# Reading back a block of Z in three transfers instead of two: 48 rows on SP's queue, 4 rows on GpSimd's

## The chip, the core and the metric

The kernel runs on one core of a Trainium2 chip. The metric is the device time of one execution, in microseconds (us), as the median of several runs. A core has engines that run side by side: TensorE (PE, with weight loads shown as PEld), VectorE (DVE), ScalarE (ACT), GpSimd (POOL) and SyncE (SP). Each has a queue of its own instructions in program order. Transfers are issued from SP's or from GpSimd's queue here, and they are carried out by 16 DMA engines that both queues share.

## What is computed

The reference chains two layers. The first is a long causal convolution of `x` (8 batches, 5696 positions, 128 channels) with a filter `h` for each channel, by FFT of twice the length. The second takes that result's first 64 frequencies through a complex matrix each, transforms back, adds, and applies a channel matrix with a ReLU:

```
Xf = rfft(x, n=2S);  Hf = rfft(h, n=2S);  y = irfft(Xf * Hf, n=2S)[:, :S]      # S = 5696
X  = rfft(y);  Y[:, m] = X[:, m] @ (w_r[m] + i w_i[m])  for m < 64, else 0
u  = y + irfft(Y, n=S)
out = u + max(u @ w_ch, 0)
```

## The kernel before

The transform of length S is split as 64 x 89. The batches go in four pairs `g_`. For each pair, the first part of the kernel transforms `x`, multiplies it with the filter's spectrum and applies the short inverse transform. What comes out, called Z, has 180 rows (90 frequencies, a real and an imaginary row each), 64 positions, and 2 x 128 columns (two batches by channels), in 16-bit floats. The function `tick` does four frequencies at a time and writes each step's Z to a scratch tensor in HBM (`zscr`) from SP's queue; the transfers carry the token `("zd", g_, s_)`. It also keeps sums for the 64 modes of the second layer.

The second part of the kernel reads Z back in blocks. A block is one pair and 16 of the 64 positions: 180 rows of 8192 bytes. There are 16 blocks. As an SBUF tile has 128 partitions, a block is two tiles: `zt[i % NC][0]` with rows 0 to 127, and `zt[i % NC][1]` with the other `RB` = 52 rows, which lie in partitions 32 to 83 (`PB` = 32). Five blocks have a buffer at a time (`NC` = 5); the profile calls them ZT0a, ZT0b to ZT4a, ZT4b.

- `load_zt` (L527 to 533) reads one block: a transfer for each part, both on SP's queue, on the semaphores of the ring `"t"`. It waits until what lay in the buffer's memory before is no longer read: in the first round older tensors (`zt_old`), later PE's matmuls on the block that had the buffer.
- `clear_zt` (L535) sets partitions 0 to 31 of the second tile to zero on GpSimd, once for each buffer, since PE reads its partitions 0 to 83.
- The first four blocks are loaded during the last pair's ticks, by the table `early` (L558 to 565): memset 0 at tick 9, load 0 at tick 10, memset 1 at tick 14, load 1 at tick 16, load and memset 3 at tick 19, load and memset 2 at tick 21. After the last tick come `load_wi` (two small transfers on GpSimd's queue, the tile WI), then load and memset 4. Block `i + 5` is loaded when block `i` has been used (L923).
- `u_z` (L782) has PE multiply a block with the transform's last matrix: for each of 16 positions and two batches a matmul with the first part and one with the second, 89 columns wide, accumulated in PSUM. `u_c` (L809) adds the second layer's contribution in a 356-column matmul (tiles IBs, C). `u_tile` copies the sum to the tile UT on ACT or DVE.
- `o_tile` (L866) multiplies UT with `w_ch` and the identity (tile WI, four 256-column matmuls), ACT takes the ReLU into R, DVE adds it into an output buffer O (seven of them of 512 KB, two tiles each) or Os, and SP's queue stores it to `out`. The main loop (L913) interleaves blocks and output tiles: while PE works on one pair's blocks, output tiles of the pair before are made.

The order of the work comes from a recorder (`Recorder`). Each instruction names the tokens that it reads and writes; the recorder works out which earlier instructions it must wait for, and puts the waits ahead of it on its engine. A transfer's semaphore comes from a ring of a fixed length (`"t"` 20, `"q"` 10; the ring `"q"` exists before the change and is not used). Waiting holds up all that stands behind on the same queue. The helpers `dma` (L319) and `mm` (L322) record transfers and matmuls, so that most rows of the profile carry L320 and L323, and it is the tile names that tell them apart.

Of the kernel before, what the change touches and what calls it, by code (L numbers as in the profile page):

```python
# [4 lines left out]
P = 128  # L5
# [118 lines left out]
def bass_long_conv_fft__then__afno_spectral_mix_kernel(nc, x, h, moe_w_r, moe_w_i, moe_w_ch, out):  # L124
# [10 lines left out]
    NT = (NK + KT - 1) // KT  # L135
# [22 lines left out]
    s4 = np.stack([back[:, None, None] * np.cos(ang), -back[:, None, None] * np.sin(ang)], axis=0)  # L158
    RB, PB = 2 * NK - P, 32
# [46 lines left out]
    def at(name, cols, dt, off):  # L206
        return nc.alloc_sbuf_tensor_at(name, [P, cols], dt, offset=off)
# [49 lines left out]
    NC = 5  # L257
    ZP = ZB * 2 * D
# [5 lines left out]
    zt = [[at(f"ZT{i}{'ab'[p_]}", ZP, F16, zt_off[i][p_]) for p_ in range(2)] for i in range(NC)]  # L264
# [27 lines left out]
    def pv(bank, off, dims, p0=0, n=P):  # L292
        return bass.AP(ps, p0 * 4096 + bank * 512 + off, [[4096, n]] + [list(d) for d in dims])
# [5 lines left out]
    def bank(i):  # L299
        return ("bank", i)  # L300
# [18 lines left out]
    def dma(eng, dst, src, ring, reads=(), writes=(), after=()):  # L319
        R.add(eng, lambda h_: h_.dma_start(dst, src), reads, writes, ring=ring, after=after)  # L320

    def mm(o, l, r, st, sp, reads, writes):  # L322
        R.add("tensor", lambda h_: h_.matmul(o, l, r, start=st, stop=sp), reads, writes)  # L323
# [3 lines left out]
    def once(key, toks):  # L327
        if key in first:
            return []
        first[key] = 1  # L330
        return list(toks)
# [3 lines left out]
    def turns(name, items):  # L335
        i = ring2.get(name, 0)
        ring2[name] = i + 1
        return items[i % len(items)]
# [102 lines left out]
    for j in range(16):  # L441
        t = turns("h", [0, 2, 4])
# [11 lines left out]
        if j % 2:  # L454
            i = j // 2 % 2 * XC + j // 4
# [69 lines left out]
    zt_old = [(H_ALL, H_ALL), (AST, AST), (AST, AST), (H_ALL, H_ALL), (M_ALL[3:6], G_ALL)]  # L525

    def load_zt(i):  # L527
        g_, c_ = divmod(i, J // ZB)
        for part, (p0, r0, n) in enumerate(((0, 0, P), (PB, P, RB))):
            old = list(once(("zt", i % NC, part), zt_old[i % NC][part]))  # L530
            dma("sync", bass.AP(zt[i % NC][part], p0 * ZP, [[ZP, n], [1, ZP]]),
                bass.AP(zs, (g_ * 2 * NK + r0) * J * 256 + c_ * ZB * 256, [[J * 256, n], [1, ZP]]),
                "t", [("zd", g_, s_) for s_ in range(NT)], [("zt", i % NC, part)], after=old)

    def clear_zt(i):  # L535
        z32 = zt[i][1][0:PB, :].bitcast(U32)
# [14 lines left out]
    def load_s4(part):  # L551
# [6 lines left out]
    early = {3: lambda: load_w(2), 5: lambda: load_w(3), 8: lambda: load_s4(1),  # L558
             9: lambda: clear_zt(0),
             10: lambda: load_zt(0),  # L560
             12: lambda: load_s4(0),
             14: lambda: (load_id(), load_ib(), clear_zt(1)),
             16: lambda: load_zt(1),
             19: lambda: (load_zt(3), clear_zt(3)),
             NT - 2: lambda: (load_zt(2), clear_zt(2))}
    pace = []
# [211 lines left out]
    NCH = J // ZB  # L778
# [3 lines left out]
    def u_z(i, b, half, alone=False, parts=(0, 1)):  # L782
        g_, c_ = divmod(i, NCH)
        t = ahead.get((i, b, half))
        if t is None:
            t = turns("l", LSLOT)
        z = zt[i % NC]
        for hb in parts:
            if not alone:
                u_c(i, b, half, t, hb, True)  # L790
            for pl in range(4):
                for ri in range(2):
                    pz = half * 8 + hb * 4 + pl
                    so = (c_ * ZB + pz) * NQ
                    n = (P, PB + RB)[ri]
                    mm(pv(t + hb, pl * NQ, [[1, NQ]]), z[ri][0:n, pz * 256 + b * P:pz * 256 + b * P + P], s4_sb[ri][0:n, so:so + NQ],
                       alone and pl == 0 and ri == 0, not alone and pl == 3 and ri == 1, [("zt", i % NC, ri), ("zt0", i % NC), ("s4", ri, 0)] + ([("s4", ri, 1)] if c_ >= NCH // 2 else []), [bank(t + hb)])
        if alone:
            ahead[(i, b, half)] = t
        return t  # L800

    def u_c(i, b, half, t, hb, first_):
        g_, c_ = divmod(i, NCH)
        pl0 = half * 8 + hb * 4
        mm(pv(t + hb, 0, [[1, 4 * NQ]]), c_sb[:, (2 * g_ + b) * P:(2 * g_ + b + 1) * P],
           ib_sb[:, (c_ * ZB + pl0) * NQ:(c_ * ZB + pl0 + 4) * NQ], first_, not first_,
           [("c", g_ // 2), ("ib", 0)] + ([("ib", 1)] if c_ >= NCH // 2 else []), [bank(t + hb)])

    def u_tile(i, b, half):  # L809
        g_, c_ = divmod(i, NCH)  # L810
        t = ahead.get((i, b, half))
        if t is None:
            t = u_z(i, b, half)
        else:
            for hb in range(2):
                u_c(i, b, half, t, hb, False)
        ub = (g_ % 2) * 2 + b
        old = {0: WT, 1: WT, 2: U_ALL, 3: U_ALL}[ub]
        n_ev[0] += 1
        e = "scalar" if n_ev[0] % 8 in (0, 2, 3, 5, 7) or g_ == NP - 1 else "vector"  # L820
        src = pv(t, 0, [[1, NQ], [512, 2], [NQ, 4]])
        evac(bass.AP(u_sb[ub], c_ * ZB + half * 8, [[S, P], [J, NQ], [4, 2], [1, 4]]),
             src, [bank(t), bank(t + 1)], [("u_", ub, 2 * c_ + half)], eng=e, after=once(("u", ub), old))
# [6 lines left out]
    def mix(m0, m1):  # L830
        for m in range(m0, m1):
            for ri, first_col in ((0, (3 * m + 1) * B), (1, 3 * m * B)):
                n = min(MC, 32 - m % 32)
                mm(pv(6 + m // 32, m % 32 * 2 * B, [[1, 2 * B * n]]), w_sb[:, (ri * M + m) * D:(ri * M + m + 1) * D],
                   bass.AP(xt, first_col, [[B * XTW, P], [0, n], [1, 2 * B]]), ri == 0, ri == 1, WT + XTT, [bank(6 + m // 32)])

    u_z(0, 0, 0, True)
    for n in range(2):
        mix(16 * n, 16 * n + 16)
        u_z(0, 0, 1, True, (n,))  # L840
    mix(32, M)
    u_z(0, 1, 0, True, (0,))
    for hb in range(2):
        evac(bass.AP(y_sb, hb * 32 * B, [[2 * M * B, P], [B, 32], [M * B, 2], [1, B]]),
             pv(6 + hb, 0, [[2 * B, 32], [B, 2], [1, B]]), [bank(6 + hb)], [("y", hb)], eng="vector" if hb else "scalar",
             after=ZY)
# [66 lines left out]
    for g_ in range(NP):  # L913
        last = g_ == NP - 1
        order = [(c_, b) for b in range(2) for c_ in range(NCH)] if last else [(c_, b) for c_ in range(NCH) for b in range(2)]
        for n, (c_, b) in enumerate(order):
            i = NCH * g_ + c_
# [46 lines left out]
```

## Time and profile before

| what | value |
|---|---|
| runs, median of 3 | 378.18 us (377.16 to 381.03) |
| the profiled execution's own time | 379.06 us |
| its span | 377.3 us |
| granted TensorE clock, mean | 0.995 |
| PE busy | 359.0 us, 95% of the span |
| DVE, ACT, POOL busy | 295.1, 314.7, 75.4 us |
| moved by DMA | 103.94 MB, mean 276 GB/s |
| issues for blocks of Z | 32, all on SP's queue: 16 of 1024 KB, 16 of 416 KB |

The span runs from the first to the last instruction of one profiled execution, and the execution's own time holds what lies around it too. In the timeline, the line of an issue gives the time that the issue took on its queue; the time to landing is given apart, where the profile can find it. A wait is put down to what released it; "issue" stands where the profile can't tell. Busy time of PE is modelled for matmuls that overlap, so two matmuls' starts say more than their durations.

In the span, the transform of the filter and of the first inputs takes the first 40 us or so, and the four pairs follow. The last writes of Z are issued from 262.50 us on, within 3.33 us. Blocks of Z are issued from 236.85 to 327.92 us, PE reads them from 257.1 to 364.4 us, and the last store is issued at 373.8 us.

### The profile page before, as it was taken

The numbers are of one execution on the slowest core, as the hardware profiler recorded it, in microseconds if no ns is written. First come the engines' busy times: TensorE is split into PE (matmuls) and PEld (weight loads), VectorE is DVE, ScalarE is ACT, GpSimd is POOL, SyncE is SP. The second block draws the span as 40 slices with busy tenths as digits, with TensorE's granted clock in tenths as the row PEclk, the third lists the DMA queues.
The fourth block names the chain that finished last, engine by engine and source line by source line (L and its number), as shares of the span: only waits on it lengthen the run. The fifth ranks groups of instructions, "written<-read, shape, count | busy, mean of one in ns | idle before, by whom it ended". The sixth has DMA issues, their size and how long they took to land.

```text
span 377.3 us, 12488 instructions
## 1 busy us (share of the span) xinstructions
PE 359.0 (95%) x5370; PEld 279.0 (74%) x5370; DVE 295.1 (78%) x336; ACT 314.7 (83%) x495; POOL 75.4 (20%) x117
## 2 busy tenths in 40 slices
PE   7989989999999999999999999999999999999994
PEld 7878856666866666866667856667899989888873
DVE  3548889998898999998998988873547767756666
ACT  8468779998999997989997999996557677688885
POOL 8803011200552320743220401124000000000000
PEclk9998999999999999999999999999999999999999
DMA  7999959987899997899996899999999999999978
GB/s 145 209 289 363 242 148 200 264 214 225 130 159 197 221 265 221 95 144 207 256 261 178 85 292 344 336 364 351 366 408 394 414 418 407 414 404 384 362 303 343
DMA packets 87048, 103.94 MB, mean 276 GB/s; under 512 B 22730, under 2 KB 72522, under 8 KB 83438
## 3 DMA queue, kind: packets, MB, share of 16 engines
q1 hardware_dynamic: 64610, 81.33, 61.3%
q0 software_dynamic: 22384, 21.83, 35.0%
q8 instruction: 42, 0.69, 0.7%
q14 instruction: 12, 0.10, 0.1%
HBM read 70.61 MB, written 51.12 MB: 323 GB/s over the span
## 4 chain that ended last, share of the span: by engine, by line
PE 60%; ACT 15%; DMA 9%; DVE 7%; issue 4%; POOL 3%; SPq 1%; DVEq 0%; ACTq 0%; POOLq 0%
PE ps L323 60%; ACT As L313 7%; DMA out_dram<-O 4%; DMA Xr<-in_x_dram 4%; ACT Zs L311 2%; DVE As L317 2%; ACT Xs L311 2%; POOL Xr L320 2%; ACT Zt L311 2%; ACT R L896 1%; DMA Hs<-Hs 1%; DVE Xin L365 1%; POOL Hin L320 1%; DVE U L655 1%; DVE U L622 1%
## 5 line engine op out<-in xcount | busy, mean ns | idle before, releaser
L655 DVE TENSOR_TENSOR U<-Xs,Hs 128x2048 f16<-128x2048 f16 (+1 forms) x73 | 86.6, 1192 | 13.9 <-ACT Xs L311 12.9
L323 PE MATMUL ps<-U,Wc 128*128 128x512 f16 (+1 forms) x368 | 94.0, 376 | 1.4 <-DVE U L622 1.4
L311 ACT CAST Xs<-ps 128x1024 f16<-128x1024 f32 (+1 forms) x77 | 74.8, 978 | 9.9 <-PE ps L323 6.9
L311 ACT CAST Zs<-ps 128x512 f16<-128x512 f32 (+1 forms) x132 | 69.1, 594 | 1.7 <-PE ps L323 1.7
L897 DVE TENSOR_TENSOR O<-ps,R 128x512 f32<-128x512 f32 x81 | 52.3, 684 | 20.7 <-ACT R L896 11.3
L317 DVE TENSOR_SCALAR As<-ps 128x720 f16<-128x720 f32 (+1 forms) x67 | 55.8, 881 | 6.7 <-PE ps L323 5.2
L896 ACT ACTIVATE R<-ps 128x512 f32<-128x512 f32 (+1 forms) x92 | 50.5, 591 | 8.7 <-PE ps L323 8.6
L323 PE MATMUL ps<-F,Xin 128*128 128x180 f16 x512 | 53.5, 254 | 3.9 <-DVE Xin L365 2.4
L323 PEld LDWEIGHTS ps<-F,Xin 128*128 128x128 f16 x512 | 45.8, 155 | 11.2 <-DVE As L317 3.3
L323 PE MATMUL ps<-As,M 64*128 64x128 f16 (+2 forms) x1488 | 51.9, 215 | 1.3 <-ACT As L313 1.2
L313 ACT ACTIVATE As<-ps 128x720 f16<-128x720 f32 (+1 forms) x65 | 46.1, 768 | 8.2 <-PE ps L323 7.6
L323 PE MATMUL ps<-WI,UT 128*128 128x256 f16 x360 | 50.9, 278 | 0.5 <-ACT UT L311 0.4
L323 PEld LDWEIGHTS ps<-U,Wc 128*128 128x128 f16 x368 | 28.6, 97 | 30.3 <-ACT Zs L311 3.7
L311 ACT CAST UT<-ps 128x712 f16<-128x712 f32 x46 | 34.5, 752 | 18.2 <-PE ps L323 17.0
L323 PEld LDWEIGHTS ps<-As,M 64*128 64x128 f16 x1488 | 41.6, 94 | 7.6 <-ACT As L313 1.7
L323 PEld LDWEIGHTS ps<-WI,UT 128*128 128x128 f16 x360 | 39.0, 152 | 3.4 <-issue 1.8
L323 PE MATMUL ps<-IBs,C 128*128 128x356 f16 x128 | 39.2, 314 | 0.5 <-DVE O L897 0.4
L320 POOL DMA_DIRECT2D Xt<-in_x_dram x40 | 21.5, 542 | 80.5 <-PE ps L323 80.0
L323 PEld LDWEIGHTS ps<-G,Zs 128*128 128x128 f16 x512 | 26.1, 96 | 14.5 <-ACT Zs L311 2.0
L655 DVE TENSOR_TENSOR U<-ps,Hs 128x2048 f16<-128x2048 f32 x15 | 34.3, 2284 | 0.0
L323 PE MATMUL ps<-G,Zs 128*128 128x128 f16 (+2 forms) x512 | 32.2, 192 | 0.1
L311 ACT CAST Zt<-ps 128x512 f16<-128x512 f32 x52 | 28.5, 622 | 0.2 <-PE ps L323 0.2
(74 smaller groups left out, 483.1 us busy)
## 6 DMA issues: line engine op xcount, KB each, us to landing
out_dram<-O SPq DMA_DIRECT2D x39, 512.0 KB, 9.9
zscr<-Zs SPq DMA_DIRECT2D x62, 256.0 KB, 6.1
zscr<-Zt SPq DMA_DIRECT2D x26, 256.0 KB, 6.3
Xt<-in_x_dram POOLq DMA_DIRECT2D x20, 320.0 KB, 7.0
W<-wscr SPq DMA_DIRECT2D x4, 1024.0 KB, 7.7
ZT0a<-zscr SPq DMA_DIRECT2D x4, 1024.0 KB, 10.3
M<-cM POOLq DMA_DIRECT2D x5, 720.0 KB, 16.8
ZT1a<-zscr SPq DMA_DIRECT2D x3, 1024.0 KB, 11.0
```

The lines of the kernel that those rows point to most:

```text
L311: R.add(e, lambda h_: h_.copy(dst, src), reads, writes, after=after)
L313: R.add(e, lambda h_: h_.activation(dst, src, COPY, scale=scale), reads, writes, after=after)
L317: R.add(e, lambda h_: h_.tensor_scalar_mul(dst, src, scale), reads, writes, after=after)
L320: R.add(eng, lambda h_: h_.dma_start(dst, src), reads, writes, ring=ring, after=after)
L323: R.add("tensor", lambda h_: h_.matmul(o, l, r, start=st, stop=sp), reads, writes)
L365: R.add("vector", lambda e: e.tensor_copy(bass.AP(x_sb, i * XN * XS, [[XW, NQ], [XS, XN], [1, D]]), src), list(toks) + XZ, [("xin", i)])
L622: R.add("vector", lambda e: e.tensor_tensor(bass.AP(u_s[0], b * 512 + d0, [[2048, P], [1024, 2], [D, n], [1, d1 - d0]]), bass.AP(s_[0], s_ ...
L655: R.add("vector", lambda e: e.tensor_tensor(uv, src, hv, MULT), bk + [("h", t, 0), ("h", t, 1, 0), ("h", t, 1, J)], [("u", i)])
L896: R.add("scalar", lambda e: e.activation(rv, src_r, RELU), bk, [("r", i % NR)], after=once(("r", i % NR), G_ALL + XTT + [("y", 0), ("y", 1 ...
L897: R.add("vector", lambda e: e.tensor_tensor(ov, src_u, rv, ADD), bk + [("r", i % NR)], [key + (h_,)], after=once(key, old))
```

## The change

The second part's transfer is cut in two. 48 of the 52 rows (`RE`, the largest multiple of 16) go as before on SP's queue and the ring `"t"`, into partitions 32 to 79. The last 4 rows go in a transfer of their own into partitions 80 to 83, issued from GpSimd's queue, right after the second one in the program, on the ring `"q"`. The third piece has its own token, `("zt", buffer, 2)`. It waits for the same things as the second part. PE's matmuls on the second part read both tokens, so the first of them in a block waits for both transfers. `clear_zt`, `early` and all else stay.

```
     def load_zt(i):
         g_, c_ = divmod(i, J // ZB)
-        for part, (p0, r0, n) in enumerate(((0, 0, P), (PB, P, RB))):
-            old = list(once(("zt", i % NC, part), zt_old[i % NC][part]))
-            dma("sync", bass.AP(zt[i % NC][part], p0 * ZP, [[ZP, n], [1, ZP]]),
+        RE = RB // 16 * 16
+        for part, (p0, r0, n) in enumerate(((0, 0, P), (PB, P, RE), (PB + RE, P + RE, RB - RE))):
+            t_, more = min(part, 1), part == 2
+            old = list(once(("zt", i % NC, part), zt_old[i % NC][t_]))
+            dma("gpsimd" if more else "sync", bass.AP(zt[i % NC][t_], p0 * ZP, [[ZP, n], [1, ZP]]),
                 bass.AP(zs, (g_ * 2 * NK + r0) * J * 256 + c_ * ZB * 256, [[J * 256, n], [1, ZP]]),
-                "t", [("zd", g_, s_) for s_ in range(NT)], [("zt", i % NC, part)], after=old)
+                "q" if more else "t", [("zd", g_, s_) for s_ in range(NT)], [("zt", i % NC, part)], after=old)
```

In `u_z`, the list of tokens that a matmul reads:

```
-    [("zt", i % NC, ri), ("zt0", i % NC), ("s4", ri, 0)] + ...
+    [("zt", i % NC, r_) for r_ in range(2 * ri, 3 * ri + 1)] + ([("zt", i % NC, 1)] if ri else []) + [("zt0", i % NC), ("s4", ri, 0)] + ...
```

For the first part (`ri` = 0) that is token 0, for the second (`ri` = 1) tokens 1 and 2 (and a token 3 that nothing writes).

More of the change, by code (lines that the diff above doesn't have):

```diff
@@ L796, in u_z @@
                     mm(pv(t + hb, pl * NQ, [[1, NQ]]), z[ri][0:n, pz * 256 + b * P:pz * 256 + b * P + P], s4_sb[ri][0:n, so:so + NQ],
-                       alone and pl == 0 and ri == 0, not alone and pl == 3 and ri == 1, [("zt", i % NC, ri), ("zt0", i % NC), ("s4", ri, 0)] + ([("s4", ri, 1)] if c_ >= NCH // 2 else []), [bank(t + hb)])
+                       alone and pl == 0 and ri == 0, not alone and pl == 3 and ri == 1, [("zt", i % NC, r_) for r_ in range(2 * ri, 3 * ri + 1)] + ([("zt", i % NC, 1)] if ri else []) + [("zt0", i % NC), ("s4", ri, 0)] + ([("s4", ri, 1)] if c_ >= NCH // 2 else []), [bank(t + hb)])
         if alone:
```

## The prediction

> **What bounds the kernel now.** I read the page's 40 slices first, then the busy time by stage, the waits from 257 us on, the chain of waits in order of time, the DMA issues, and the timelines of PE and SP. All blocks of Z are issued between 237 and 329 us and used between 257 and 365 us, so only that part of the span can answer to the change. By stages:
>
> ```profile
> core 0: us, PE busy (x) PEld busy (x) DVE busy (x) ACT busy (x) POOL busy (x), PEclk, DMA share, GB/s
> 257.00:282.00 25.00, 24.20 (x476) 21.65 (x477) 10.91 (x13) 13.03 (x17) 2.04 (x2) 1.00 1.03 375
> 282.00:330.00 48.00, 47.95 (x687) 43.18 (x685) 35.49 (x54) 34.91 (x61) 0.00 (x0) 1.00 1.01 409
> 330.00:345.00 15.00, 15.00 (x203) 13.09 (x202) 8.96 (x16) 13.00 (x23) 0.00 (x0) 1.00 0.99 396
> 345.00:373.50 28.50, 26.28 (x292) 21.74 (x290) 21.11 (x35) 24.54 (x44) 0.00 (x0) 1.00 0.87 348
> ```
>
> Two things are full at once from 257 to 345 us: PE (in the timeline its 89-column matmuls start every 0.04 us) and the DMA engines (share 0.99 to 1.03). What tells them apart is who waits for whom. From 257 us on, the waits that a DMA ended are these two; the third line is what the profile can't assign:
>
> ```profile
> DVE O L897 <- issue: 3.1, 6, 0.7
> ...
> DVE O L897 <- DMA out_dram<-O: 0.3, 1, 0.3
> ...
> PEld ps L323 <- DMA ZT2b<-zscr: 0.2, 1, 0.2
> ```
>
> So PE is the bound and DMA only just keeps up. The chain has one DMA on it, and it is a store, not a load: a store of 15.85 us holds its output buffer, DVE waits for it, and PE for DVE.
>
> ```profile
> 326.98 0.90 SPq L320
> ...
> 327.92 0.99 SPq L320
> ...
> 328.96 15.85 DMA out_dram<-O
> ...
> 344.93 0.70 DVE O L897
> 345.63 0.14 issue
> 345.77 4.28 PE ps L323 x53
> ```
>
> Why does a 512 KB store take 15.85 us, when the median store takes 9.9? The DMA issues hold the hint:
>
> ```profile
> out_dram<-O SPq DMA_DIRECT2D x39, 512.0 KB, 9.9
> ...
> ZT0a<-zscr SPq DMA_DIRECT2D x4, 1024.0 KB, 10.3
> ...
> ZT0b<-zscr SPq DMA_DIRECT2D x4, 416.0 KB
> ...
> Xh<-in_x_dram POOLq DMA_DIRECT2D x4, 320.0 KB, 12.6
> ...
> WI<-in_moe_w_ch_dram POOLq DMA_DIRECT2D x1, 32.0 KB, 8.0
> ```
>
> The 128-row part (ZT0a) has a time to landing, the 52-row part (ZT0b) has none. The trace has 16 completion marks for each store and each first part, 14 for each second part: one right after the issue (issue 237.45, mark 238.04), when no data can be there, and 13 with data. I read 52 rows as 13 engines with 4 rows each and three engines with none. The store issued at 328.96 supports that: its first mark is at 334.32, its last at 344.81, so some engines are 10.5 us ahead of the others. For ZT0's first part, issued at 236.85, the spread was 242.07 to 244.06, only 2.0 us. Thirteen engines collect a backlog and three don't.
>
> **The change part by part.** The sum is made against the profiled execution: 379.06 us, of which 377.3 are span and 1.8 lie around it. The median of the runs is 378.18, so 0.9 is taken off at the end.
>
> *48 rows on SP.* The second part's last mark comes 1.23 us after the first part's (ZT0: 279.28 and 280.51), for 4 rows of 8 KB on each engine: 0.31 us a row. Per block the 13 busy engines now move 8 + 4 = 12 rows, the others 8. With 48 rows over 16 engines it is 8 + 3 = 11 on all, and 4 rows more on some: 11.25 on average. The busy ones are relieved of 0.75 x 0.31 = 0.23 us per block. At ZT2's first load (the fourth block issued) that is 0.9 us, at the last block 16 x 0.23 = 3.7 us.
>
> What that is worth is what PE loses to DMA now:
>
> ```profile
> 270.72 0.20 PE L323 MATMUL ps<-S4a,ZT2a 128*128 128x89 f16 x1
> 270.86 0.21 PE L323 MATMUL ps<-S4b,ZT2b 84*128 84x89 f16 x1
> ...
> 344.50 1.06 PE L323 MATMUL ps<-WI,UT 128*128 128x256 f16 x8
> 345.77 0.31 PE L323 MATMUL ps<-IBs,C 128*128 128x356 f16 x1 [0.20 <-DVE O L897]
> ```
>
> First place: from 270.72 to 270.86 is 0.14, where neighbours start 0.04 apart: 0.10 us lost. ZT2's second part landed at 270.82; 0.9 earlier is 269.9, ahead of its use. Second place: from 344.50 to 345.77 is 1.27 us; the same eight matmuls one tile later (346.75 to 347.65) take 0.90: 0.37 lost. The store would land at 344.81 - 3.5 = 341.3, and DVE would start when its data are there, near 344.6. Next late after that is nothing from DMA: the following stores' buffers have 0.6 us or more of slack now, and would have over 4. Sum: -0.10 - 0.37 = -0.47 us. As bounds: 0 if nothing lands earlier, and -3.6 if the 3.1 us of unassigned DVE waits are stores as well. I take -0.47, because by the stores' marks every other output buffer was free 0.6 us or more before DVE wrote it.
>
> *4 rows on GpSimd.* Sixteen issues more. GpSimd's own 36 KB loads take about 0.52 us each to issue: 8.3 us, all on a queue that is idle after 259.1 us (POOL busy is 0.00 in the later rows above). The five early ones queue with other work: the pieces of ZT0 and ZT1 stand behind their buffers' memsets, those of ZT3, ZT2 and ZT4 before theirs, and the two WI loads (256.13 and 256.69) behind ZT2's. Each waits for what the memset beside it waits for as well, so what is queued behind slips by some 0.5 us each. The memsets' rows are needed 12 us later or more, WI landed by 264.67 and is used at 279.49. I cost this at nothing; without that cover it would be 5 x 0.5 = 2.6 us once. On the DMA engines its 4 rows are the quarter row per engine counted above.
>
> *SP.* The count of issues stays 32 for Z. Its issues last 0.4 to 2.4 us while the engines are backed up; SP only holds stores back there, and the store after ZT0 went 0.3 us after its data were ready (DVE done 328.65, issue 328.96). Nothing is taken.
>
> *A wait more on PE.* The first matmul on each block's second part now waits for two transfers. Behind it on PE everything is queued. A separate wait costs:
>
> ```profile
> L115 PEldq EVENT_SEMAPHORE  x105: 51/51/1171, 27.0 to 371.5; - x105
> ```
>
> So 16 x 0.051 = 0.8 us if none is hidden, and 0 if all are. One such at 278.565 (beside ZT4's first use) left the matmuls at their usual 0.15 and 0.04 apart, since the weight load runs ahead under a 356-column matmul. That is the nearest row: I take 0.
>
> Whole sum: 379.06 - 0.47 = 378.59 in the profiled execution's terms, 378.18 - 0.47 = **377.7 us** against the median: no change that can be told from the scatter.
>
> **The rivals.**
>
> *A. Balancing lands nothing earlier*, because all engines together are at a limit, not each one. For: the share is over 0.99 with three engines partly idle. Against: stores in the tail, where all 16 engines work, end 1.25 us apart (348.17, 349.39, 350.66) for 32 KB per engine, about what ZT0's second part takes on 13 engines for its 32 KB (1.23), so each engine has its own pace. The time would be 378.2. [...]
>
> *B. GpSimd's four rows come last* (slower). PE needs both pieces at a block's first second-part matmul, and one late piece stops PE, then ACT, DVE and the stores. It is issued when the buffer is free. The least room is ZT2's: GpSimd had ZT2 free at 254.4, PE needs it at 270.8, 16 us. Block 5: free at 266.6, needed at 285.4, 19 us; later ones 21 to 26. It decides from 16 us of flight on. At 20 us the time is 4 us longer, once, since the later blocks move along: 382. Against: GpSimd's flights here are 5.7 and 8.0 us (WI, into this very backlog) and 12.6 at the worst median (Xh). [...]
>
> *C. Waits that the profile can't assign are DMA's* (faster). The 3.1 us of DVE O above and the 0.47 would go: 378.18 - 3.6 = 374.6. Against: the buffers were free by the stores' marks.
>
> **How the numbers follow.** Forecast 0.60, A 0.22, B 0.11, C 0.07. What a measurement of this kernel can tell from no change is about 1%, 3.8 us: the runs before spread from 377.16 to 381.03. Forecast and A are inside that; B is past it for flights of 20 us and more; C is inside except for its upper end. So faster 0.05, same 0.84, slower 0.11. The range: below, the lowest run less the sum and less one unassigned wait, 377.16 - 0.47 - 0.7 = 376.0; above, the median with all 16 PE waits paid and the profiled run's surplus, 378.18 + 0.8 + 0.9 = 379.9, and halfway into B, to 380.6. Below and above that lie C and the rest of B, under 2 in 10.
>
> **What would show it.** Right: the 48-row parts get a time to landing (16 marks); the first and last mark of late stores lie 2 to 4 us apart, not 10; the wait of DVE O on a store and the one of PE on ZT2b are gone; PE's eight WI matmuls at 344 take 0.9 us; PE starts by tile unchanged. Wrong: landings as late as before (A); waits of PE that end with a ZT piece of GpSimd's queue (B); DVE O's unassigned waits shrinking by microseconds (C); or PE's starts slipping by 0.05 us at each block (the extra wait), up to 0.8 us.

## The result, and the profile after

The changed kernel takes 396.17 us (median of 6 runs, 394.04 to 399.29) against 378.58 us (6 runs, 377.16 to 381.03): 1.0475 times as long, 95% interval 1.0437 to 1.0513. The forecast was 377.7 us, no change, in a range of 376.0 to 380.6. It was wrong, and by a mechanism that none of its rivals held. Medians here and below are of all runs, while a ratio leaves out runs more than 1.5% above the fastest of their kernel (two of four in "Both pieces on SP", one of four in "Four up").

The profiled execution took 394.77 us with a span of 393.0. PE reads its first block of Z at 257.1 us in both kernels, and its last at 364.4 us before and 380.2 us after. That difference, 15.8 us, is all of the difference of the two executions (394.77 - 379.06 = 15.7). So the loss lies in the stage that reads Z, as the prediction placed it. By stages, after:

```profile
257.00:282.00 25.00, 19.23 (x372) 16.82 (x373) 9.03 (x10) 9.34 (x11) 3.82 (x5) 0.93 1.06 305
282.00:330.00 48.00, 45.41 (x643) 40.48 (x640) 29.77 (x45) 31.53 (x53) 3.57 (x8) 0.96 1.02 342
```

The columns are those of the table shown before. The reader should look at the last two. The DMA share is about what it was (1.06 and 1.02, before 1.03 and 1.01), but the rate is 305 and 342 GB/s, where it was 375 and 409. The DMA engines are as busy as before and move 19% and 16% less. PE (19.23 and 45.41 us busy, before 24.20 and 47.95) now has gaps, and the mean granted clock of the two stages is 0.93 and 0.96, before 1.00.

The DMA issues show who became late, and the new landing time of the second part:

```profile
out_dram<-O SPq DMA_DIRECT2D x39, 512.0 KB, 14.6
...
ZT0a<-zscr SPq DMA_DIRECT2D x4, 1024.0 KB, 16.0
...
ZT0b<-zscr SPq DMA_DIRECT2D x4, 384.0 KB, 16.8
...
ZT0b<-zscr POOLq DMA_DIRECT2D x4, 32.0 KB, 6.6
```

Stores went from 9.9 to 14.6 us, ZT0's unchanged 128-row part from 10.3 to 16.0. GpSimd's four rows are quick, 6.6 us. What PE loses is seen first where the cover was least, at ZT2:

```profile
270.48 0.31 PE L323 MATMUL ps<-IBs,C 128*128 128x356 f16 x1
274.84 0.21 PE L323 MATMUL ps<-S4a,ZT2a 128*128 128x89 f16 x1 [4.05 <-DMA ZT2a<-zscr]
275.98 0.25 PE L323 MATMUL ps<-S4b,ZT2b 84*128 84x89 f16 x1 [0.93 <-DMA ZT2b<-zscr]
```

That is 5.3 us more than the usual starts (0.15 and 0.04 us apart). GpSimd's piece of that block had landed at 260.61; it is SP's parts that came at 274.79 and 275.93. The first part landed at 269.61 before, so it is 5.2 us late. Of these, 3.4 us were lost before its issue, on SP's queue, where the issue of ZT3's first part took 3.28 us instead of 0.50:

```profile
256.40 3.28 SPq L320 DMA_DIRECT2D ZT3a<-zscr  x1
...
262.78 1.33 SPq L320 DMA_DIRECT2D ZT2a<-zscr  x1
```

```profile
255.10 0.50 SPq L320 DMA_DIRECT2D ZT3a<-zscr  x1
...
259.35 0.65 SPq L320 DMA_DIRECT2D ZT2a<-zscr  x1
```

(The first pair is the changed kernel's, the second that of before.) The other 1.8 us are the flight, 12.0 us instead of 10.3. Later places are stores that hold output buffers. The waits from 257 us on, and the chain of work:

```profile
DVE O L899 <- DMA out_dram<-O: 5.6, 2, 2.9
...
DVE O L899 <- issue: 1.1, 3, 0.7
```

```profile
264.16 11.78 DMA ZT2b<-zscr
275.93 0.05 issue
275.98 20.04 PE ps L323 x300
...
333.86 18.88 DMA out_dram<-O
```

The first of the two waits was 0.3 us before. From 257 us on, the distances between PE's starts, less the median that the kernel before has for the same kind of instruction, sum to 24.2 us, against 8.4: the difference of 15.8 us is the whole loss. Of the 24.2 us, 4.4 lie in three stretches of 3.4 us (from 275.6, 299.5 and 354.1 us) in which the granted clock was 0.5; before, it was 1.0 from 257 us until PE had ended. Each stretch begins within 1.5 us of the end of a PE gap of 2 us or more, which suggests that this part of the loss came with the gaps; one such gap, ending at 338.04, had no stretch behind it.

The trace keeps a record of each packet. A row of Z is one packet of 8192 bytes. Those that SP's queue issued, between 257 and 330 us, in ns:

| kernel | mean | median | 90th percentile |
|---|---|---|---|
| before | 326 | 309 | 309 |
| changed | 426 | 352 | 615 |

Before, nearly every row takes 309 ns, the 0.31 us of the prediction. After, half of them take over 352, and the 90th percentile is at twice 309. The stores' packets of 4096 bytes hardly changed (161 and 164 ns on average). So it is the rows on their way into SBUF that became slow, the 128-row part's too, which the change doesn't touch: 58% of the packets took over 312 ns (9% before), and only 48 of the 176 rows that SP's queue moves for a block are the second part's.

### The profile page after: what moved, and what is told of

The parts are those of the page before. It is cut to its first block, busy times and chain, and to the rows that moved or that the text cites. A ratio compares the mean times of both kernels' runs of the same rounds, so it can differ in the third digit from the quotient of the medians.

```text
span 393.0 us, 12518 instructions
## 1 busy us (share of the span) xinstructions
PE 361.7 (92%) x5370; PEld 279.6 (71%) x5370; DVE 296.0 (75%) x336; ACT 315.0 (80%) x495; POOL 83.5 (21%) x133
## 4 chain that ended last, share of the span: by engine, by line
PE 57%; DMA 20%; ACT 10%; DVE 5%; issue 3%; POOL 3%; SPq 1%; DVEq 0%; POOLq 0%; ACTq 0%
PE ps L323 57%; ACT As L313 6%; DMA out_dram<-O 5%; DMA Xt<-in_x_dram 4%; DMA Xr<-in_x_dram 4%; DMA ZT2b<-zscr 3%; DMA zscr<-Zt 3%; DVE As L317 2%; POOL Xr L320 2%; DMA zscr<-Zs 2%; DVE U L624 1%; SPq L320 1%; POOL Hin L320 1%; ACT Xs L311 1%; ACT Zt L311 1%
## 5 line engine op out<-in xcount | busy, mean ns | idle before, releaser
L323 PE MATMUL ps<-F,Xin 128*128 128x180 f16 x512 | 52.3, 250 | 3.9 <-DVE Xin L365 2.5
L323 PE MATMUL ps<-WI,UT 128*128 128x256 f16 x360 | 52.6, 284 | 2.4 <-DVE O L899 1.9
L323 PEld LDWEIGHTS ps<-F,Xin 128*128 128x128 f16 x512 | 44.5, 155 | 11.3 <-DVE As L317 3.2
L323 PE MATMUL ps<-IBs,C 128*128 128x356 f16 x128 | 40.5, 324 | 2.2 <-DVE O L899 2.1
L323 PEld LDWEIGHTS ps<-G,Zs 128*128 128x128 f16 x512 | 26.0, 96 | 14.6 <-ACT Zs L311 2.0
## 6 DMA issues: line engine op xcount, KB each, us to landing
out_dram<-O SPq DMA_DIRECT2D x39, 512.0 KB, 14.6
```

## The experiments

Three theories were put up against each other. **P** (place): engines that write into SBUF at the same time can hold each other up, and the partitions that their rows go to decide whether they do. The 52 rows at 32, with four rows on each of 13 engines, are a place where the packets took 309 ns (median); three rows on each of 16 engines, or the same 52 rows elsewhere, need not be. That engines hold each other up is an assumption, which the 90th percentile of 615 ns, about twice 309, would fit: no record names the engine of a packet, so a run can test the place alone. **H**: all 16 engines reading Z at once collide at the source. **Q**: GpSimd's queue disturbs the engines.

**Moved two partitions up.** The kernel before, and nothing but the place of the 52 rows changed (34 to 85):

```
-    RB, PB = 2 * NK - P, 32
+    RB, PB = 2 * NK - P, 34
```

> The kernel before, with its second part's 52 rows two partitions further up (34 to 85 instead of 32 to 83): same queue, same 13 engines with 4 rows each, same bytes, same source rows. [...] By P this run is slow like the changed kernel: 388 to 400 us, GB/s in the Z stage near 340 at a DMA share near 1.0. Theory H (all 16 engines read Z at once and collide at the source): no change, 378 to 380. Theory Q (a second queue's transfers slow the engines): no change, 378 to 380.

Measured: 396.6 us, 1.0438 (1.0368 to 1.0507). Slow, as P has it (334 and 362 GB/s in the two stages), with the queue, the rows' source and the bytes unchanged. But the edit did one thing more: the factors' tile S4b now had 86 rows, and its load landed at 246.3 instead of 238.9 us, with 3 completion marks. PE's first use of a block slipped to 260.9. So it was repeated further down.

**Both pieces on SP.** The change, with `"sync"` for the third piece:

```
-            dma("gpsimd" if more else "sync", bass.AP(zt[i % NC][t_], p0 * ZP, [[ZP, n], [1, ZP]]),
+            dma("sync", bass.AP(zt[i % NC][t_], p0 * ZP, [[ZP, n], [1, ZP]]),
```

> The change with both pieces, 48 rows and 4 rows, on SP's queue. Q: back to 378 to 381 us, as nothing of Z goes through GpSimd. P: slow, 388 to 400, since the 48 rows lie over the 16 engines as in the changed kernel. H: slow as well, 388 to 400.

Measured: 399.28 us, 1.0459 (1.0373 to 1.0544). GpSimd's queue isn't needed for the loss: Q falls as its main cause.

**GpSimd's four rows alone.** 52 rows whole on SP, and 4 spare rows on GpSimd:

```
-        for part, (p0, r0, n) in enumerate(((0, 0, P), (PB, P, RE), (PB + RE, P + RE, RB - RE))):
+        for part, (p0, r0, n) in enumerate(((0, 0, P), (PB, P, RB), (PB + RB, P + RE, RB - RE))):
```

> The kernel before with its 52 rows whole on SP, and besides a transfer of 4 rows on GpSimd for each block into partitions 84 to 87, which no matmul reads; PE waits for it as in the change. It is the GpSimd half of the change alone. Q: slow, 388 to 400 us. P: only 4 rows of a block collide in one group of partitions, 378 to 383. H: 378 to 381.

Measured: 383.05 us, 1.0123 (1.0089 to 1.0157), at the upper end of what P gives (378 to 383).

**64 rows, four for each of 16 engines.** The second part with 12 rows more, in partitions 32 to 95; its factors for those 12 are zero:

```
-    RB, PB = 2 * NK - P, 32
+    RB, PB, PX = 2 * NK - P, 44, 12
...
-        for part, (p0, r0, n) in enumerate(((0, 0, P), (PB, P, RB))):
+        for part, (p0, r0, n) in enumerate(((0, 0, P), (PB - PX, P - PX, RB + PX))):
...
```

> [...] P: no collisions, 377 to 381 us, with packets as fast as before although 23% more bytes go in the second part. H: all 16 engines read at once as in the changed kernel or worse, 390 to 405 us. Q: 378 to 381.

Measured: 378.28 us, 0.9997 (0.9977 to 1.0017). This is the experiment that ends H: all 16 engines read, more bytes are moved, and the time is that of before. The stage, with the columns as above:

```profile
282.00:330.00 48.00, 47.68 (x677) 42.86 (x675) 35.66 (x54) 34.59 (x60) 0.00 (x0) 1.00 1.02 420
```

The share of 1.02 now carries 420 GB/s; the changed kernel's same 1.02 carries 342. The 8 KB packets average 317 ns (309 at the 90th percentile).

**Two up, without the side effect.** As the first, with S4b's load at 128 rows:

```
-        n = PB + RB if part else P
+        n = P
```

> The first experiment again, without its side effect: two partitions further up, the factors' tile S4b had 86 rows and its one load came late (246 instead of 239 us, and PE's first use of a block 3.8 us later). Here that load takes 128 rows (the rest are zeros). 52 rows at partitions 34 to 85, on 13 engines. Theory P (two engines in one group of partitions): first use of ZT0 back near 257 us, and still 388 to 394 us, as the last experiment less 3.8 and a bit. If the side effect was the cause: 378 to 381.

Measured: 391.7 us, 1.0313 (1.0252 to 1.0375).

```profile
282.00:330.00 48.00, 47.89 (x698) 42.66 (x695) 33.26 (x49) 33.85 (x57) 0.00 (x0) 1.00 1.00 361
```

A share of 1.00 at 361 GB/s, and packets of 378 ns on average, 533 at the 90th percentile. PE's first use of ZT0 came at 258.5 us, 1.35 later than in the kernel before, which is a small part of the loss. Where the rows lie in SBUF is enough by itself.

**Four up.** `PB` = 36 and the same load of S4b: the same 52 rows, at partitions 36 to 87. The author took it that no two engines of one transfer meet there, which no run shows.

> [...] Two forms of P: if only two engines of the same transfer collide, 378 to 381 us. If an engine also collides with another engine's stores and first parts, because the engines are at different transfers at a time, slower: 383 to 396.

Measured: 399.58 us, 1.0526 (1.0468 to 1.0583): slower than two up, and slower than the 383 to 396 us that P's second form gave.

```profile
282.00:330.00 48.00, 42.97 (x610) 38.21 (x608) 28.58 (x42) 29.54 (x50) 0.00 (x0) 0.96 1.00 320
```

320 GB/s, packets of 443 ns on average. The slow end lies at twice 309 ns: 10.6% of them took 600 to 640 ns and 3.6% took longer. So P's first form, 378 to 381 us, failed, and its second, with collisions between different transfers, gave too little. Both are the author's estimates: no trace here shows two engines collide.

**The four rows to HBM.** As the experiment with 4 spare rows, but they end in a scratch tensor:

```
-            dma("gpsimd" if more else "sync", bass.AP(zt[i % NC][t_], p0 * ZP, [[ZP, n], [1, ZP]]),
+            dma("gpsimd" if more else "sync", bass.AP(sp, i % NC * 4 * ZP, [[ZP, n], [1, ZP]]) if more else bass.AP(zt[i % NC][t_], p0 * ZP, [[ZP, n], [1, ZP]]),
...
```

> As the experiment with 4 spare rows on GpSimd (383.1 us), but the 4 rows go to a scratch tensor in HBM instead of partitions 84 to 87. PE waits for them still. P: no group of partitions is written, back to 378 to 380. Q (the second queue as such, its issues and PE's wait): stays at 382 to 384.

Measured: 379.93 us, 1.0035 (1.0008 to 1.0063). Sixteen issues on GpSimd, their traffic and PE's wait cost 0.35%; the same rows into four partitions cost 1.23%.

**48 rows alone.**

```
-        for part, (p0, r0, n) in enumerate(((0, 0, P), (PB, P, RB))):
+        for part, (p0, r0, n) in enumerate(((0, 0, P), (PB, P, RB // 16 * 16))):
...
-                    n = (P, PB + RB)[ri]
+                    n = (P, PB + RB // 16 * 16)[ri]
```

> The 48 rows on SP alone; the last 4 rows of Z's 180 are left out, so part of the sum over frequencies is missing and PE's matmuls read 80 partitions. It is the other half of the change. P: the greater part of the loss, 388 to 394 us. If the 4-row pieces were the main cost: 378 to 383.

Measured: 392.06 us, 1.0339 (1.0288 to 1.039). With the four rows' 1.23% that makes 4.6%, near the change's 4.75% (two measured ratios added; that they add is an assumption).

**Partitions 0 to 51.** `PB` = 0, S4b's load at 128 rows, the memset at partitions 64 to 95.

> 52 rows at partitions 0 to 51 on SP, with the 128-row load of S4b; GpSimd's memset goes to partitions 64 to 95, which nothing reads. [...] If any aligned place but 36 were good: 378 to 380.

Measured: 564.03 us, 1.4879 (1.4807 to 1.495), and not for DMA's sake. The loads land long before use; the DMA share is 0.32. PE's matmuls:

```profile
299.87 0.25 PE L323 MATMUL ps<-S4b,ZT2b 52*128 52x89 f16 x1
300.06 0.26 PE L323 MATMUL ps<-S4a,ZT2a 128*128 128x89 f16 x1
300.25 0.25 PE L323 MATMUL ps<-S4b,ZT2b 52*128 52x89 f16 x1
```

They start 0.19 us apart instead of 0.04, at a granted clock of 0.50, which this run had from 260.4 to 530.1 us. The edit had cut the rows of every second matmul from 84 to 52. Before 260.4 us the clock was still 1.00, and there the rows alone can be read:

```profile
257.50 0.21 PE L323 MATMUL ps<-S4b,ZT0b 52*128 52x89 f16 x1
257.65 0.21 PE L323 MATMUL ps<-S4a,ZT0a 128*128 128x89 f16 x1
257.80 0.21 PE L323 MATMUL ps<-S4b,ZT0b 52*128 52x89 f16 x1
```

The starts are 0.145 us apart at full clock. As a test of P the run is void.

**All 52 rows on GpSimd.** At partitions 32 to 83:

```
-            dma("sync", bass.AP(zt[i % NC][part], p0 * ZP, [[ZP, n], [1, ZP]]),
+            dma("gpsimd" if part else "sync", bass.AP(zt[i % NC][part], p0 * ZP, [[ZP, n], [1, ZP]]),
...
-                "t", [("zd", g_, s_) for s_ in range(NT)], [("zt", i % NC, part)], after=old)
+                "q" if part else "t", [("zd", g_, s_) for s_ in range(NT)], [("zt", i % NC, part)], after=old)
```

> The 52 rows whole, at partitions 32 to 83 as before, but all of them issued from GpSimd's queue. Q (the second queue): 384 us or more. P, if a transfer from GpSimd's queue is dealt to the engines as one from SP's (4 rows on each of 13): 377 to 380. [...]

Measured: 379.41 us, 1.0032 (1.0007 to 1.0056). Sending 52 of Z's 180 rows through the second queue costs 0.3%, and its packets take 314 ns on average. So the queue by itself isn't what slows the rows. That these 52 rows go to 13 engines as on SP's queue shows in the stores: three of their marks are still early (336.88, 336.92 and 337.20 for the one issued at 330.21, the fourth at 339.15).

**Partitions 0 to 51, matmuls of 84 rows.** The void one mended:

```
+        if i < NC:
+            dma("sync", bass.AP(zt[i][1], RB * ZP, [[ZP, 64 - RB], [1, ZP]]), c_zero.ap(), "q", (), [("zt", i, 2)],
+                after=list(once(("zt", i, 2), zt_old[i][1])))
...
-                    n = (P, PB + RB)[ri]
+                    n = (P, 84)[ri]
...
```

> The last but one experiment (52 rows at partitions 0 to 51, 564 us) without its side effect: there PE's matmuls read 52 partitions instead of 84 and started 0.19 us apart instead of 0.04, at a granted clock of 0.5. Here they read 84 again: partitions 52 to 63 are filled with zeros once for each buffer by five transfers of 12 rows, 64 to 95 by GpSimd's memset. [...] If any place but 32 is as bad: 395 to 402. [...]

Measured: 396.94 us, 1.0464 (1.0395 to 1.0534); packets of 425 ns on average, 615 at the 90th percentile. It is slow, so partition 0 is a bad place too, and nearly as bad as 36 (1.0464 against 1.0526). The time lies where "any place but 32 is as bad" put it. The author's estimate from P, 384 to 394 us, was too low; it took for granted which engine writes which partitions, and that was not shown. The five zero transfers land up to 0.5 us after the block's other rows at ZT2 and can explain only part. What makes 0 nearly as bad as 36 wasn't tried.

## Why the prediction was wrong, point by point

- **What bounds the kernel**: right. PE and the DMA engines are both full (from 282 to 330 us PE busy 47.95 of 48.00 us, DMA share 1.01), with next to no cover. ZT2 went first, and a store that holds an output buffer is on the chain again (18.88 us, before 15.85).
- **52 rows are 13 engines of 4, 48 are 16 of 3**: borne out by the marks, as far as they tell of engines. On SP's queue 52 rows have 14 marks, one of them right after the issue, and S4b's 84 rows have 15, of which one is early as well. With 48 rows the second part has 16 marks and a landing time. GpSimd's four-row pieces have 16 marks too, so marks alone don't tell how many engines carry rows there. The change spread its 48 rows over all 16 engines and lost 4.75%; the run with 64 rows on 16 engines lost nothing (0.9997).
- **0.31 us a row, whatever the split: the step that failed.** The sum took the row's price from 13 engines with 4 rows and gave it to 16 with 3. The first and last mark of late stores did draw together (the one issued at 333.86 had 346.51 and 352.74, 6.2 us apart, not 10.5, where 2 to 4 was forecast), but at a mean of 426 ns a row all engines were late. The upper bound of that term was set at 0, "if nothing lands earlier". No row excluded that rows get slower. They did in this run, and the experiments with the rows moved in SBUF show that the place alone can do it (378 ns and 1.0313 for two partitions up).
- **The gain of 0.47 us**: its two places became losses, ZT2 by 5.3 us. The 64-row transfer, which gives all engines work at 309 ns, shows what balance can be worth: 0.9997 (0.9977 to 1.0017), nothing that can be told.
- **GpSimd's issues and PE's wait cost nothing**: nearly; with the pieces' traffic to HBM they cost 0.35% with interval 0.08 to 0.63%, or about 1.3 us, where 0 to 0.8 was the bound for the wait.
- **SP, at which nothing was taken**: this failed as a consequence. SP did not hold back stores alone; it issued ZT2's first part 3.4 us late, and that is most of the 5.2 us by which it landed late.
- **Rival A** was right that nothing lands earlier, not why: the 64-row run reached 420 GB/s, so there was no limit on all engines together at 409. **Rival B** had the sign and the place, PE at ZT2, but not the cause: GpSimd's piece was there 15 us before SP's. **Rival C**: the unassigned waits of DVE O shrank from 3.1 to 1.1 us while the time rose.
- **The range** reached 380.6, since every term had been bounded by how late something could be, and none by how slow it could become.

What is shown: moving the 52 rows to another place in SBUF slows the 8 KB packets (326 ns on average with the rows at 32, 378 at 34, 443 at 36), with the same queue, source and bytes; and 48 rows over 16 engines slow them too (48 rows alone: 1.0339), although they lie where they lay before. The number of engines alone isn't it, as 64 rows over 16 engines lost nothing (317 ns). So the good cases are 52 rows at 32 and 64 rows at 32, and the bad ones 52 rows at 34, 36 and 0, and 3 rows an engine. What tells them apart was not shown, for no record names the engine of a packet or what held it up. Twice 309 ns at the slow end would fit two engines that take turns, which stays an inference. No run gave 16 engines three rows each at another place, so it stays open whether three rows an engine cost something by themselves.

## What to carry to other kernels

Before a transfer is split or moved, measure its packets at the new place and under the new spread. Here the 8 KB packets of that stage averaged 326 ns with the 52 rows at partition 32 and 443 ns with them at 36, and an uneven spread of 52 rows over 13 engines beat an even one of 48 rows over 16 (the changed kernel took 1.0475 times as long). A row's price that was read under one spread need not hold under another, so bound it on both sides. When the DMA share is near 1, read it with GB/s: here the same share at a lower rate meant that packets got slower, not that there was more to move.

## What the runs showed of the hardware that was not expected

- Small loads can cost by where they go. Sixteen of 32 KB, four rows for each block into four partitions, cost 1.23% (0.89 to 1.57%), into HBM 0.35%.
- 86 rows were loaded with 3 completion marks, 15 us after the issue, where 84 rows took 7.6 us with 15 marks.
- Matmuls of 52 rows that alternate with ones of 128 started 0.145 us apart at a granted clock of 1.00, and 0.19 at 0.50. With 84 rows it was 0.04 us at 1.00, and 0.074 at 0.50 (in the changed kernel's three stretches at that clock). So most of it is the shape, not the clock.
